# Chunked RWKV recurrence with a fused MLP: pair products and inverses turned by VectorE, and a first state product with 32 stationary columns

## Chip, cores and metric

The kernel runs on one core of one Trainium2 chip. The metric is device time in microseconds (us), the median over repeated runs of the whole kernel, which is one launch.

## What is computed

The reference runs a recurrence over 768 time steps for each of 4 x 8 = 32 heads, with a 40 x 40 state per head, and then a two-layer MLP on the result. Cut to what matters:

```python
for t in range(S):                                          # S = 768
    y[:, :, t] = np.einsum('bhd,bhde->bhe', rt, state)
    Sa = np.einsum('bhde,bhe->bhd', state, at)
    state = state * wt[:, :, None, :] - np.einsum('bhd,bhe->bhde', Sa, bt)
    state = state + np.einsum('bhd,bhe->bhde', vt, kt)
x = y.transpose(0, 2, 1, 3).reshape(B * S, H * D)           # 3072 x 320
h = x @ w_in                                                # 320 x 2048
g = np.where(h >= 1, h, np.where(h <= -1, 0, (h + 1) ** 2 / 4))
return g @ w_out                                            # 2048 x 320
```

All inputs and outputs are float32.

## The kernel before

**The recurrence in chunks.** Time is cut into 24 chunks `c` of 32 steps. Inside a chunk, the products of every step's `a` with every step's `b` form a strictly triangular 32 x 32 matrix per head (the *pair products*). With the inverse of one plus that matrix, a chunk needs only matrix products. Four chunks make a *stage* `s` (six stages), so that pair products and inverses are made for 128 (head, chunk) pairs at once, one per partition.

**Making the pair products and the inverses.** `prelude(s)` multiplies up the decays and writes the scaled rows of k, a, b and the decay product to the DRAM scratch `scr` (the *rows*); for stages 0 and 1 `early_products` does so up front. `ab_set(s)` (`early_ab` for stages 0 and 1) forms the pair products on TensorE, 32 x 32 blocks with time in the partitions, and ScalarE copies them out of PSUM (L206, L303). Then they go to the DRAM tensor `abd` by four DMAs per copy (L208, L306) and come back with one (head, chunk) pair per partition (L316, `lw<-abd`). `invert(s)` runs the elimination: 31 pairs of a multiply (L326) and a subtract (L332) on tile `lw`, on VectorE for stage 0 and on GpSimd for the others. The inverse `W` is written to DRAM tensor `ttd` (L335) and read back, 32 x 32 per head with time in the partitions, into the columns `C_T` of the working tile `cg` (L409, part 1 of `load_cg`, which first drains the stage's inversion: its instructions are written out at the latest there).

**The chain.** `chain(c, hb)` handles a half chunk: 16 of the 32 heads, and 48 of them in all. It has five steps of 16 small products each, on TensorE: L468 (here *the first product*: stationary are the 64 columns of inverse and scores in `cg`, contraction over all 128 partitions, 72 moving columns; ScalarE copies the result to `x0` by L473 in two copies), L479 (*the second product*: the inverse, 32 x 32, times `x0`), L497, L526 and L536. Two half chunks are interleaved. Beside them stand `scores` (L438) and the VectorE transpositions of `turn` (L423, L426, L428), which read rows that `load_ti` brings from `scr` (L274). `load_cg` (L398, L401) brings the other rows.

**The MLP.** Its products (L607 first layer, L581 and L585 second layer) are fed between the chain's steps, 3 x 1024 moving columns per step, from the chunks already done; the correction `gl` (L595) comes from GpSimd.

**What sets the order.** It is written out by hand: the loop at the end takes the chain's steps, ten per chunk, and after each step `background` advances rows, pair products and inversion of the coming stages by the table `WINDOWS`, in counted steps. Inversion of stage 1 has the window from step 16 to 36, the next ones 53 to 72, 90 to 112, 129 to 152 and 170 to 192. Chunk 4 (the first of stage 1) begins at step 40, but its first `load_cg`, with the drain, stands at the start of chunk 3, at step 30. All DMAs but a few go out on SyncE's queue (SP), in program order. Each engine works in order too.

**Before the loop.** Stage 0 is inverted on VectorE, with its output needed by the first half chunk. The order written there is `early_products(0)`, `early_turn(0)`, `early_ab(0)`, the first step of `invert(0)`, `early_products(1)`, and then a loop that takes one inversion instruction at a time with the early work of stage 1 and the first scores between.

Of the kernel before, what the change touches and what calls it, by code (L numbers as in the profile page):

```python
# [23 lines left out]
C_T, C_X, C_R, C_S, C_G, CW = 0, 32, 64, 96, 136, 176  # L24
# [25 lines left out]
def rwkv_moe_kernel(ctx: ExitStack, tc: tile.TileContext, r, k, v, w, a, b, w_in, w_out, ident_d, mask_d, out):  # L50
# [44 lines left out]
    abd = [dram.tile([2, 4, NH // 2, L, L], F32, name=f"abd{s}") for s in range(NS)]  # L95
    ttd = [dram.tile([2, 4, NH // 2, L, L], F32, name=f"ttd{s}") for s in range(NS)]
# [43 lines left out]

    early_rows = {}
# [48 lines left out]
    def early_ab(s, half):  # L190

        ps = psum()
        if half == 0:
            early_rows[s] = work.tile([128, 16, 2, 32], F32, tag="ea", name="ea").rearrange("p a b x -> p (a b x)")
        ab = early_rows[s][:, 512 * half : 512 * half + 512]
# [10 lines left out]
        nc.scalar.copy(ab, ps)  # L206
# [69 lines left out]
    def ab_set(s):  # L276
# [6 lines left out]
        for c in range(4 * s, 4 * s + 4):  # L283
# [18 lines left out]
            ab = work.tile([128, 8, 32], F32, tag="ab", name="ab")  # L302
            nc.scalar.copy(ab, ps[:, 0:256].rearrange("p (s x) -> p s x", x=32))  # L303
            yield AB_W[2]
            for q in range(4):
                nc.sync.dma_start(  # L306
                    abd[c // 4][q // 2, c % 4, q % 2 :: 2].rearrange("h t i -> t h i"), ab[32 * q : 32 * q + 32]
                )
            yield AB_W[3]

    def invert(s):
# [4 lines left out]
        nc.sync.dma_start(Lm, abd[s].rearrange("f c h t i -> (f c h) (t i)"))  # L316
# [4 lines left out]
        L3 = Lm.rearrange("p (t i) -> p t i", i=32)  # L321
# [12 lines left out]
        yield 2  # L334
        nc.sync.dma_start(ttd[s].rearrange("f c h t i -> (f c h) (t i)"), W)  # L335
        yield 3
# [13 lines left out]

    done, size, spent = dict(rows=1, ab=1), dict(rows=10 + 4 * (6.2 + sum(ROWS_W)), ab=AB_W[4] + 4 * (4 * AB_W[0] + sum(AB_W[1:4])), inv=INV_W + 67), {}
# [38 lines left out]
    def load_cg(c, hb, parts=(0, 1)):  # L390
        cg = cgs[(2 * c + hb) % 3]
        hsel = slice(16 * hb, 16 * hb + 16)
        if 0 in parts:
            drain("rows", c // 4)
# [59 lines left out]
    def chain(c, hb):  # L454
# [11 lines left out]
        for h in range(16):  # L466
# [5 lines left out]
            if h % 8 == 7:  # L472
                nc.scalar.copy(x0[:, halves[h // 8]], psv[h // 8][:, :, 0:72])  # L473
# [297 lines left out]
    for hb in range(2):  # L771
        load_ti(0, hb)
        load_cg(0, hb, (0,))
# [152 lines left out]
```

## Time and profile before

| | before |
|---|---|
| runs, us | 974.76, 976.89, 983.64 (median 976.89) |
| span of the profiled execution, us | 974.4 |
| mean granted TensorE clock | 0.850 |
| TensorE busy | 80% |
| VectorE, ScalarE, GpSimd busy | 61%, 49%, 46% |
| DMA packets, MB | 276866, 134.64 |

The span reaches from the first to the last instruction of the program; no other time of that execution is listed. The span stands 0.4 us below the fastest of the three runs and 2.5 us below their median, so sums made against the span are carried to the median by adding 2.5.

In the profile, PE is TensorE's matmul and PEld its weight load, DVE is VectorE, ACT ScalarE, POOL GpSimd and SP SyncE; a q behind the name is the engine's sequencer, which issues DMAs. L468 is line 468 of the kernel. A float32 matmul shows as two records, so that 16 products are "x32". A group's row gives, behind the bar, busy time and the mean of one in ns. A timeline row gives start and length in us; in brackets stands the idle time ahead of it and what ended that. The chain of waits is followed back from the last instruction, at each step to what released it.

### The profile page before, as it was taken

What the parts mean: (1) busy time and instruction counts of PE and PEld (TensorE: products, weight loads), DVE (VectorE), ACT (ScalarE), POOL (GpSimd) and SP (SyncE); (2) the same over time, 40 slices, a digit from 0 to 9 for tenths busy, and PEclk for the clock granted to TensorE, in tenths of its full rate; (3) what the DMA queues carried; (4) which work ended last, traced back from release to release, by engine and by line L of the source; (5) the groups of instructions that cost most, each with busy time, mean ns of one, the idle gap of its engine ahead of it and who ended that gap; (6) DMA issues with size and microseconds to landing.
All of it is one profiled execution on the core that took longest, in us unless ns stands there. A gap on an engine that the chain in (4) does not pass through costs nothing.

```text
span 974.4 us, 35827 instructions
## 1 busy us (share of the span) xinstructions
PE 775.0 (80%) x14976; PEld 692.1 (71%) x14976; DVE 590.4 (61%) x1562; ACT 478.6 (49%) x1230; POOL 443.8 (46%) x673
## 2 busy tenths in 40 slices
PE   4523543447886988799879798989999999999995
PEld 3312532336776887688879687978898899999995
DVE  7782876574756583775654774776665556655321
ACT  5822444212543544454445454546565566656663
POOL 5200223686331599332588232697235962222332
PEclk9755555575997789797999796999999999999998
DMA  8799995565677755896735886856855545552010
GB/s 274 148 193 245 202 207 151 141 139 134 146 156 152 163 138 115 178 186 130 179 100 117 182 160 133 173 135 131 146 115 121 110 101 111 105 90 56 16 36 14
DMA packets 276866, 134.64 MB, mean 138 GB/s; under 512 B 194984, under 2 KB 266856, under 8 KB 276704
## 3 DMA queue, kind: packets, MB, share of 16 engines
q1 hardware_dynamic: 273504, 121.20, 57.9%
q0 software_dynamic: 3200, 11.14, 3.8%
q8 instruction: 118, 1.93, 0.9%
q14 instruction: 44, 0.36, 0.1%
HBM read 96.83 MB, written 33.82 MB: 134 GB/s over the span
## 4 chain that ended last, share of the span: by engine, by line
PE 34%; DMA 16%; POOL 16%; DVE 12%; issue 8%; SPq 8%; ACT 4%; POOLq 0%; ACTq 0%; DVEq 0%
PE ph L607 11%; PE po L581 6%; POOL lw L326 5%; POOL lw L332 4%; DMA ti<-scr 4%; PE po L585 3%; PE p L497 3%; POOL gl L595 3%; SPq L274 3%; PE p L468 3%; PE p L526 2%; DMA ld_a<-in_a_dram 2%; PE p L438 2%; PE p L479 2%; PE p L536 1%
## 5 line engine op out<-in xcount | busy, mean ns | idle before, releaser
L607 PE MATMUL ph<-X,w 120*128 120x256 f32 x1536 | 260.9, 307 | 51.6 <-DVE qt L620 44.3
L595 POOL TENSOR_TENSOR gl<-qt,gh 128x256 fp32r<-128x256 f32 x192 | 140.9, 734 | 280.0 <-ACT gh L594 264.6
L607 PEld LDWEIGHTS ph<-X,w 120*128 120x128 f32 x1536 | 219.8, 203 | 68.1 <-DVE qt L620 51.3
L620 DVE SCALAR_TENSOR_TENSOR qt<-qt,ph 128x256 f32<-128x256 f32 x192 | 79.9, 416 | 150.3 <-ACT qt L614 148.3
L581 PE MATMUL po<-wide,gh 128*128 128x320 f32 x768 | 163.7, 329 | 0.3 <-ACT gh L594 0.3
L594 ACT CAST gh<-qt 128x256 fp32r<-128x256 f32 x192 | 78.0, 406 | 167.6 <-DVE qt L620 166.7
L581 PEld LDWEIGHTS po<-wide,gh 128*128 128x128 f32 x768 | 124.6, 202 | 3.7 <-ACT gh L594 0.5
L613 ACT ACTIVATE qt<-ph,half_c 128x256 f32<-128x256 f32 x192 | 91.1, 474 | 53.4 <-POOL gl L595 39.7
L585 PE MATMUL po<-wide,gl 128*128 128x320 f32 x384 | 99.6, 338 | 17.6 <-POOL gl L595 17.6
L497 PE MATMUL p<-cg 128*64 128x72 f32 (+1 forms) x1536 | 74.8, 262 | 44.2 <-DVE cg L486 39.7
L497 PEld LDWEIGHTS p<-cg 128*64 128x64 f32 x1536 | 66.8, 166 | 54.3 <-ACT cg L490 45.0
L326 POOL TENSOR_TENSOR lw<-lw 128x31 f32<-128x31 f32 (+15 forms) x155 | 94.4, 609 | 18.0 <-DMA lw<-abd 9.3
L490 ACT ACTIVATE cg<-p 32x160 f32<-32x160 f32 x192 | 56.8, 296 | 87.9 <-DVE cg L486 61.0
L447 DVE TENSOR_TENSOR cg<-p,mask 32x256 f32<-32x256 f32 x192 | 80.6, 420 | 25.8 <-PE p L438 23.2
L332 POOL TENSOR_TENSOR lw<-lw 128x31 f32<-128x31 f32 (+15 forms) x155 | 84.1, 543 | 8.8
L504 DVE SCALAR_TENSOR_TENSOR cg<-p,pr 40x160 f32<-40x160 f32 x184 | 59.1, 321 | 41.1 <-PE p L497 39.2
L614 ACT ACTIVATE qt<-qt 128x256 f32<-128x256 f32 x192 | 80.2, 418 | 6.1
L585 PEld LDWEIGHTS po<-wide,gl 128*128 128x128 f32 x384 | 65.6, 197 | 23.9 <-POOL gl L595 21.5
L468 PE MATMUL p<-cg 128*64 128x72 f32 x1536 | 66.4, 243 | 16.7 <-DMA cg<-ttd 15.0
L486 DVE SCALAR_TENSOR_TENSOR cg<-p,mask 32x128 f32<-32x128 f32 x192 | 55.2, 288 | 36.2 <-PE p L479 30.7
L468 PEld LDWEIGHTS p<-cg 128*64 128x64 f32 x1536 | 58.7, 149 | 23.6 <-issue 19.0
L526 PE MATMUL p<-ident,cg 40*64 40x40 f32 x1472 | 57.1, 238 | 1.9 <-issue 1.9
(104 smaller groups left out, 1027.9 us busy)
## 6 DMA issues: line engine op xcount, KB each, us to landing
ti<-scr SPq DMA_DIRECT2D x96, 200.0 KB
ti<-scr SPq DMA_DIRECT2D x96, 168.0 KB
scr<-arena POOLq DMA_DIRECT2D x16, 640.0 KB, 5.4
cg<-scr SPq DMA_DIRECT2D x96, 80.0 KB
X<-Y SPq DMA_DIRECT2D x36, 160.0 KB
scr<-wide SPq DMA_DIRECT2D x8, 640.0 KB
tiab<-scr SPq DMA_DIRECT2D x32, 160.0 KB
scr<-in_r_dram SPq DMA_DIRECT2D x24, 160.0 KB
```

The costliest lines, as they stand in the source:

```text
L326: eng.tensor_mul(t3, W3[:, 0:n, j : j + 1].broadcast_to([128, n, m]), L3[:, j + 1 :, j].unsqueeze(1).broadcast_to([128, n, m]),)
L332: eng.tensor_sub(W3[:, 0:n, j + 1 :], W3[:, 0:n, j + 1 :], t3)
L447: nc.vector.tensor_tensor(out=cg[q, f::2, C_X : C_X + 64][:, 4 * i : 4 * i + 4].rearrange("p h (j x) -> p h j x", x=32), in0=ps[quarter(f, ...
L468: nc.tensor.matmul(psv[h // 8][64 * (1 - f) : 64 * (1 - f) + 64, h // 2 % 4, 0:72], lhsT=cg[:, h, C_T : C_T + 64], rhs=cg[:, h, C_R : C_R ...
L497: nc.tensor.matmul(psv[h // 8][64 * f : 64 * f + 64, h // 2 % 4, 0:n3], lhsT=cgw[:, h * CW + C_G : h * CW + C_G + 64], rhs=cg[:, h, C_R : ...
L581: nc.tensor.matmul(pos[i], lhsT=gh[:, ts_], rhs=w2[f // 8][:, j, f % 8, :], start=f == 0 and j == 0, stop=False)
L585: nc.tensor.matmul(pos[i], lhsT=gl[:, ts_], rhs=w2[f // 8][:, 0, f % 8, :], start=False, stop=f == NF - 1)
L595: nc.gpsimd.tensor_sub(gl, gt, gh.bitcast(F32))
L607: nc.tensor.matmul(ph, lhsT=w1[:, wi, fs], rhs=Xs[g][:, xi, :], start=i == 0, stop=i == 7)
L613: nc.scalar.activation(gt, ph, AF.Relu, bias=half_c, scale=0.5)
L614: nc.scalar.activation(gt, gt, AF.Square)
L620: nc.vector.scalar_tensor_tensor(out=gt, in0=gt, scalar=1.0, in1=ph, op0=ALU.min, op1=ALU.max)
```

## The change

The pair products stay in SBUF: ScalarE copies them into one tile `pairs` (time in the partitions, 32 blocks of 32), and one VectorE transposition of 128 x 1024 (32 x 32 blocks) puts a (head, chunk) pair in each partition, in `lw`. The two time indices of the matrix change places there: the elimination's multiply now reads its second operand with a step of one element, not 32. The inverse leaves `lw` by a second transposition of the same size into the tile `tinv` (in the new function `adopt`), which the second product reads as its stationary operand. `abd` and `ttd` with all their DMAs are gone, and so are the columns `C_T` of `cg`. `adopt(s)` stands at the start of the stage's first chunk (step 40 for stage 1), and the drain of the inversion with it, ten steps later than before. The first product keeps only the 32 columns that are used of its 64; its 16 results go to four quarters of 32 partitions in one PSUM tile, in place of two halves of 64 partitions in two tiles, and one ScalarE copy takes them out. The second product reads four quarters of 32 partitions, not two, and writes one PSUM tile.

```diff
-C_T, C_X, C_R, C_S, C_G, CW = 0, 32, 64, 96, 136, 176
+C_X, C_R, C_S, C_G, CW = 0, 32, 64, 104, 144
...
+    pairs = const.tile([128, 32, 32], F32, name="pairs")
+    tinv = const.tile([128, 4, 8, 32], F32, name="tinv")
+    pairs_f = pairs.rearrange("p m i -> p (m i)")
...
-        nc.scalar.copy(ab, ps)
-        for q in range(4):
-            nc.sync.dma_start(
-                abd[s][q // 2, 2 * half : 2 * half + 2, q % 2 :: 2].rearrange("c h t i -> t (c h) i"),
-                ab[32 * q : 32 * q + 32].rearrange("t (h i) -> t h i", i=32),
-            )
+        nc.scalar.copy(pairs_f[:, 512 * half : 512 * half + 512], ps)
...
-            nc.scalar.copy(ab, ps[:, 0:256].rearrange("p (s x) -> p s x", x=32))
-            yield AB_W[2]
-            for q in range(4):
-                nc.sync.dma_start(
-                    abd[c // 4][q // 2, c % 4, q % 2 :: 2].rearrange("h t i -> t h i"), ab[32 * q : 32 * q + 32]
-                )
-            yield AB_W[3]
+            nc.scalar.copy(pairs_f[:, 256 * (c % 4) : 256 * (c % 4) + 256], ps[:, 0:256])
+            yield AB_W[2] + AB_W[3]
...
-        nc.sync.dma_start(Lm, abd[s].rearrange("f c h t i -> (f c h) (t i)"))
+        nc.vector.transpose(Lm.rearrange("p (i t) -> p i t", t=32), pairs.rearrange("p m i -> p i m"))
...
-        L3 = Lm.rearrange("p (t i) -> p t i", i=32)
+        L3 = Lm.rearrange("p (i t) -> p t i", t=32)
...
-        yield 2
-        nc.sync.dma_start(ttd[s].rearrange("f c h t i -> (f c h) (t i)"), W)
-        yield 3
+        yield 5
+
+    def adopt(s):
+
+        drain("inv", s)
+        W = lw[:, 1024:2048]
+        nc.vector.transpose(tinv.rearrange("p c h i -> p i (c h)"), W.rearrange("p (a i) -> p i a", i=32))
+        turned_out.add(s)
...
-        if 1 in parts:
-            drain("inv", c // 4)
-            for f in range(2):
-                ur = 64 * (1 - f) + 32
-                tt = ttd[c // 4][f, c % 4, 8 * hb : 8 * hb + 8]
-                nc.sync.dma_start(cg[ur : ur + 32, f::2, C_T : C_T + 32], tt.rearrange("h t x -> t h x"))
...
         for h in range(16):
-            f = h % 2
+            f, p = h % 2, h // 2
+            q = 64 * f + 32 * (p % 2)
             nc.tensor.matmul(
-                psv[h // 8][64 * (1 - f) : 64 * (1 - f) + 64, h // 2 % 4, 0:72], lhsT=cg[:, h, C_T : C_T + 64],
-                rhs=cg[:, h, C_R : C_R + 72], start=True, stop=True,
-            )
-            if h % 8 == 7:
-                nc.scalar.copy(x0[:, halves[h // 8]], psv[h // 8][:, :, 0:72])
+                psv[q : q + 32, p // 2, :], lhsT=cg[:, h, C_X : C_X + 32], rhs=cg[:, h, C_R : C_R + 72],
+                start=True, stop=True,
+            )
+        nc.scalar.copy(x0, psv)
         yield
-        psv = psum_2()
-        for p in order:
-            for f in range(2):
-                q = uq[f]
-                nc.tensor.matmul(
-                    psv[p // 4][quarter(f, p // 4), p % 4, 0:72], lhsT=cg[q, 2 * p + f, C_T : C_T + 32],
-                    rhs=x0[q, p, :], start=True, stop=True,
-                )
+        psv = psum()[:, 0:288].rearrange("p (h x) -> p h x", x=72)
+        for h in range(16):
+            f, p = h % 2, h // 2
+            q = 64 * f + 32 * (p % 2)
+            nc.tensor.matmul(
+                psv[quarter(f, p % 2), p // 2, :], lhsT=tinv[q : q + 32, c % 4, 4 * hb + p // 2, :],
+                rhs=x0[q : q + 32, p // 2, :], start=True, stop=True,
+            )
...
-    for hb in range(2):
-        load_cg(0, hb, (1,))
+    adopt(0)
...
+        if 0 < c < NC and c % 4 == 0:
+            adopt(c // 4)
```

The change moves instructions on VectorE and GpSimd. The line numbers shift: in the changed kernel L303 is the transposition of the pair products, L328 that of the inverse, L314 and L320 the elimination's multiply and subtract. The first place is VectorE ahead of stage 0's inversion (`wide` and `ti` are the input and output rows of stages 0 and 1, `arena` scratch). Before:

```order
L172 TENSOR_TENSOR wide_91<-wide_90,arena 128x8x40 x4
L157 COPY wide_90<-ti_80 128x3x40
L158 TENSOR_SCALAR wide_90<-ti_80 128x40
L160 TENSOR_TENSOR wide_90<-wide_90,ti_80 128x4x40 x7
L162 TENSOR_TENSOR wide_90<-wide_90 128x8x40 x3
L167 RECIPROCAL arena<-wide_90 128x4x40
L169 TENSOR_TENSOR arena<-arena,ti_80 128x4x40 x7
L172 TENSOR_TENSOR wide_90<-tiab,arena 128x8x40 x4
L326 TENSOR_TENSOR lw<-lw 128x31
```

And in the changed kernel:

```order
L171 TENSOR_TENSOR wide_91<-wide_90,arena 128x8x40 x4
L303 STREAM_TRANSPOSE lw<-pairs 128x1024
L156 COPY wide_90<-ti_80 128x3x40
L157 TENSOR_SCALAR wide_90<-ti_80 128x40
L159 TENSOR_TENSOR wide_90<-wide_90,ti_80 128x4x40 x7
L161 TENSOR_TENSOR wide_90<-wide_90 128x8x40 x3
L166 RECIPROCAL arena<-wide_90 128x4x40
L168 TENSOR_TENSOR arena<-arena,ti_80 128x4x40 x7
L171 TENSOR_TENSOR wide_90<-tiab,arena 128x8x40 x4
L314 TENSOR_TENSOR lw<-lw 128x31
```

The transposition, which needs stage 0's pair products, stands ahead of all of stage 1's row products (25 instructions), which the DMA did not.

The second place is GpSimd at the end of stage 1's inversion (`ld_a`, `ld_b`, `ld_k`, `rec` and `arena` are rows of stage 2, `gl` is the MLP's). Before:

```order
L326 TENSOR_TENSOR lw<-lw 128x60
L332 TENSOR_TENSOR lw<-lw 128x30x2
L326 TENSOR_TENSOR lw<-lw 128x31
L332 TENSOR_TENSOR lw<-lw 128x31
L255 TENSOR_TENSOR arena<-ld_k,rec 128x8x40
L257 TENSOR_TENSOR arena<-ld_b,rec 128x8x40
L258 DMA scr_100<-arena 128x8x160
L595 TENSOR_TENSOR gl<-qt,gh 128x256
```

And in the changed kernel:

```order
L314 TENSOR_TENSOR lw<-lw 128x231
L320 TENSOR_TENSOR lw<-lw 128x21x11
L246 TENSOR_TENSOR arena<-ld_k,rec 128x8x40
L314 TENSOR_TENSOR lw<-lw 128x220
L248 TENSOR_TENSOR arena<-ld_b,rec 128x8x40
L249 DMA scr_100<-arena 128x8x160
L320 TENSOR_TENSOR lw<-lw 128x22x10
L314 TENSOR_TENSOR lw<-lw 128x207
L582 TENSOR_TENSOR gl<-qt,gh 128x256
```

The last twenty instructions of that inversion, which stood in one block ahead of the rows, now stand between them. In the later stages one instruction of GpSimd's order moves.

The third place is VectorE at the start of chunk 4 (`yt` and `pr` belong to the chain of chunk 3, `ea` to the pair products of stage 2). In the changed kernel:

```order
L496 TENSOR_TENSOR yt<-p_2678,pr_87 128x128
L496 TENSOR_TENSOR yt<-p_2679,pr_87 128x128
L607 SCALAR_TENSOR_TENSOR qt<-qt,ph_63 128x256
L415 STREAM_TRANSPOSE pr_86<-ti_81 128x16x32
L328 STREAM_TRANSPOSE tinv<-lw 128x32x32
L278 STREAM_TRANSPOSE ea<-tiab 128x256 x3
L228 TENSOR_SCALAR arena<-ld_w 128x40
```

The row of `tinv` is new, and the rest stands as before; it waits for GpSimd's last L320 of the stage.

More of the change, by code (lines that the diff above doesn't have):

```diff
@@ L139, in rwkv_moe_kernel @@
     ]
-    early_rows = {}
     def early_load(s):
@@ L192, in early_ab @@
         ps = psum()
-        if half == 0:
-            early_rows[s] = work.tile([128, 16, 2, 32], F32, tag="ea", name="ea").rearrange("p a b x -> p (a b x)")
-        ab = early_rows[s][:, 512 * half : 512 * half + 512]
         for c in (2 * half, 2 * half + 1):
@@ L301, in ab_set @@
                     )
-            ab = work.tile([128, 8, 32], F32, tag="ab", name="ab")
-            nc.scalar.copy(ab, ps[:, 0:256].rearrange("p (s x) -> p s x", x=32))
-            yield AB_W[2]
-            for q in range(4):
-                nc.sync.dma_start(
-                    abd[c // 4][q // 2, c % 4, q % 2 :: 2].rearrange("h t i -> t h i"), ab[32 * q : 32 * q + 32]
-                )
-            yield AB_W[3]
+            assert s - 1 in turned_in
+            nc.scalar.copy(pairs_f[:, 256 * (c % 4) : 256 * (c % 4) + 256], ps[:, 0:256])
+            yield AB_W[2] + AB_W[3]
     def invert(s):
@@ L388, in load_ti, with load_cg @@
         load_rows(tih[hb], c, 0, 200, 16 * hb, 16)
[L390 removed]
+    def load_cg(c, hb):
         cg = cgs[(2 * c + hb) % 3]
         hsel = slice(16 * hb, 16 * hb + 16)
[L393 to L409 removed]
+        drain("rows", c // 4)
+        sc = scr4[c // 4][c % 4][hsel]
+        for f in range(2):
+            vr, ur = 64 * (1 - f), 64 * (1 - f) + 32
+            nc.sync.dma_start(
+                cg[vr : vr + 32, f::2, C_S : C_S + 80], sc[f::2, :, O_V : O_V + 80].rearrange("h t x -> t h x")
+            )
+            nc.sync.dma_start(
+                cg[ur : ur + 32, f::2, C_G : C_G + D], sc[f::2, :, O_B : O_B + D].rearrange("h t x -> t h x")
+            )
     evs = {}
@@ L474, in chain @@
+        nc.scalar.copy(x0, psv)
         yield
-        psv = psum_2()
-        for p in order:
-            for f in range(2):
-                q = uq[f]
-                nc.tensor.matmul(
-                    psv[p // 4][quarter(f, p // 4), p % 4, 0:72], lhsT=cg[q, 2 * p + f, C_T : C_T + 32],
-                    rhs=x0[q, p, :], start=True, stop=True,
-                )
+        psv = psum()[:, 0:288].rearrange("p (h x) -> p h x", x=72)
+        for h in range(16):
[4 more added lines that the diff above has]
+                rhs=x0[q : q + 32, p // 2, :], start=True, stop=True,
+            )
@@ L483, in chain @@
         for i in range(2):
             for f in range(2):
-                q = uq[f]
+                q, j = uq[f], 1 - i
                 nc.vector.scalar_tensor_tensor(
-                    out=cg[q, f::2, C_R : C_R + 32][:, halves[i]], in0=psv[i][quarter(f, i), :, 0:32], scalar=-1.0,
+                    out=cg[q, f + 2 * i :: 4, C_R : C_R + 32], in0=psv[quarter(f, i), :, 0:32], scalar=-1.0,
                     in1=mask[quarter(f, i)].unsqueeze(1).broadcast_to([32, 4, 32]), op0=ALU.mult, op1=ALU.mult,
@@ L489, in chain @@
                 )
-                nc.scalar.mul(cg[q, f::2, C_S : C_S + D][:, halves[1 - i]], psv[1 - i][quarter(f, 1 - i), :, 32:72], -1.0)
+                nc.scalar.mul(cg[q, f + 2 * j :: 4, C_S : C_S + D], psv[quarter(f, j), :, 32:72], -1.0)
         yield
```

15 lines of the change are left out of this document (5 added, 10 removed).

## The prediction

> **What bounds the kernel now.** I read the page first: busy shares, DMA slices, and the chain of waits by engine.
>
> ```profile
> span 974.4 us, 35827 instructions
> PE 775.0 (80%) x14976; PEld 692.1 (71%) x14976; DVE 590.4 (61%) x1562; ACT 478.6 (49%) x1230; POOL 443.8 (46%) x673
> DMA  8799995565677755896735886856855545552010
> PE 34%; DMA 16%; POOL 16%; DVE 12%; issue 8%; SPq 8%; ACT 4%; POOLq 0%; ACTq 0%; DVEq 0%
> ```
>
> No engine bounds the whole: on the chain that ended last PE has a third, while DMA, SP's issuing and GpSimd have 40% together. So I split the span with the table by stretches.
>
> ```profile
> 100.00:200.00 100.00, 44.71 (x1072) 40.42 (x1069) 67.40 (x163) 37.75 (x90) 38.00 (x57) 0.59 0.78 178
> 600.00:700.00 100.00, 95.26 (x1899) 85.02 (x1898) 69.43 (x186) 54.49 (x146) 65.29 (x104) 0.96 0.66 138
> 800.00:900.00 100.00, 100.00 (x2013) 91.11 (x2012) 60.38 (x161) 62.15 (x164) 26.70 (x37) 1.00 0.45 90
> ```
>
> The first number behind the length is PE's busy time. Early, PE works 45 of 100 us at a granted clock of 0.59, with the DMA engines 78% busy: loads and order of arrival decide. From 600 on PE is busy 95% and more, at 800 without rest and at clock 1.00: there only shorter PE work helps. Third, PE's timeline of a late half chunk:
>
> ```profile
> 869.82 1.07 PEld L468 LDWEIGHTS p<-cg 128*64 128x64 f32 x32
> 869.82 1.22 PE L468 MATMUL p<-cg 128*64 128x72 f32 x32
> 870.97 0.39 PE L607 MATMUL ph<-X,w 120*128 120x256 f32 x1
> 872.92 0.48 PE L438 MATMUL p<-pr,ev 40*32 40x32 f32 x32
> 873.33 1.13 PE L526 MATMUL p<-ident,cg 40*64 40x40 f32 x32
> 875.93 0.70 PE L479 MATMUL p<-x,cg 32*32 32x72 f32 x32
> 876.57 1.22 PE L607 MATMUL ph<-X,w 120*128 120x256 f32 x8
> 883.54 0.66 PE L468 MATMUL p<-cg 128*64 128x72 f32 x14
> ```
>
> A half chunk takes 883.54 - 869.82 = 13.7 us, 2.7 us per step. A group's cost is the distance to the next start: the first product 870.97 - 869.82 = 1.15 us (36 ns per record), the second 0.64 us (20 ns) with the same 72 moving columns.
>
> **Term 1, ahead of the loop.** The timeline there:
>
> ```profile
> 18.80 0.27 DVE L157 COPY wide<-ti 128x120 f32<-128x120 f32 x1
> 27.76 0.59 ACT L206 COPY ea<-p 128x512 f32<-128x512 f32 x1 [3.49 <-PE p L202]
> 28.18 4.38 DVE L172 TENSOR_TENSOR wide<-tiab,arena 128x320 f32<-128x320 f32 x4
> 32.19 0.35 SPq L316 DMA_DIRECT2D lw<-abd  x1
> 36.23 0.21 DVE L326 TENSOR_TENSOR lw<-lw 128x31 f32<-128x31 f32 x1 [3.67 <-DMA lw<-abd]
> 72.83 0.22 DVE L332 TENSOR_TENSOR lw<-lw 128x31 f32<-128x31 f32 x1
> 73.08 0.34 SPq L335 DMA_DIRECT2D ttd<-lw  x1
> 81.42 6.70 SPq L215 DMA_DIRECT2D scr<-wide  x4
> 82.19 1.73 PE L479 MATMUL p<-x,cg 32*32 32x72 f32 x32
> 88.17 2.36 SPq L672 DMA_DIRECT2D lw<-in_moe_w_out_dram  x2
> ```
>
> Stage 1's row products ran on VectorE from 18.80 to 32.56, 13.8 us, while the pair products were made and sent. Now the transposition stands ahead of them and waits for ScalarE's copy, which ends at 28.35. What a transposition costs I take from these rows (with the elimination's, for term 4):
>
> ```profile
> L423 DVE STREAM_TRANSPOSE cg<-ti 64x256 f32<-64x256 f32 x96 | 42.0, 438 | 1.2
> L428 DVE STREAM_TRANSPOSE pr<-ti 128x512 f32<-128x512 f32 x48 | 33.6, 701 | 0.0
> L326 DVE TENSOR_TENSOR lw<-lw 128x255 f32<-128x255 f32 x2 | 1.2, 608 | 0.1
> L332 DVE TENSOR_TENSOR lw<-lw 128x255 f32<-128x255 f32 x2 | 0.8, 424 | 0.1
> L326 POOL TENSOR_TENSOR lw<-lw 128x255 f32<-128x255 f32 x10 | 7.8, 776 | 0.4
> L332 POOL TENSOR_TENSOR lw<-lw 128x255 f32<-128x255 f32 x10 | 6.8, 683 | 0.5
> ```
>
> From 256 to 512 elements 263 ns are added, so 1024 cost 701 + 2 x 263 = 1.23 us. Its operands step by 32 elements; the multiply that reads so (608 ns) runs at 1.43 times the subtract (424), so 1.8 us is the upper bound. VectorE is then free for the row products at about 29.7, and the elimination starts at 29.7 + 13.8 = 43.5, where it stood at 36.23: **7.3 us later**. It lasted 72.83 + 0.22 - 36.23 = 36.8 us. Its 31 multiplies now read contiguously; at 255 elements the two groups differ by 184 ns, at few elements by nothing, so some 4 us at most fall away: an end between 76.5 and 80.3, with the second transposition 78 to 82. Before, write and read through DRAM came next, and then the first product, which now needs no inverse: L479 stood at 82.19. On that path 0 to 4 us are won. SP wins more: it stood at L335 and behind it for the inversion, sent stage 1's rows only from 81.42 and the weights to `lw` at 88.17; the rows can now go from about 73, the weights from 80 to 82, when the second transposition has left `lw`. I take **-5** (-1 to -8).
>
> **Term 2, landings on the chain.** Two round trips stand on the chain in the loop:
>
> ```profile
> 299.24 3.21 DMA abd<-ab
> 739.36 3.65 DMA lw<-abd
> 276.15 0.75 SPq L306
> 221.16 0.71 POOL lw L326
> 231.71 0.43 POOL lw L326
> ```
>
> 3.21 + 3.65 us go; the transpositions in their place are in term 6. **-7** (0 to -7, since the next arrival may be as late).
>
> **Term 3, the first product.** With 32 stationary columns in four quarters I take the second product's row, 0.64 us: its 72 moving columns and four quarters are the same, its contraction is shorter. Saved are 0.51 us per half chunk. Where PE is the limit, from 600 to 900 us, lie 300 / 13.7 = 22 half chunks: 22 x 0.51 = **-11**. Bounds: 0 (unchanged at 1.15) and 48 x 0.51 = -24. Ahead of 600 PE idles often enough that I count nothing there. The copy to `x0` is one in place of two, but starts only behind all 16 products; I count it at nothing, since PE has the MLP's products from 870.97 until L479 starts at 875.93. Without that cover the path would gain or lose less than one copy.
>
> The Trainium skill, TensorE: Matmul & The Clock Gate, section "Part 3: Packing small matmuls — row/col tiling", says that a weight load overlaps a running matmul only when it is in other row groups, and here all quarters use all rows. By that rule the term would be 0. The trace does not agree with it for two halves: L468's weight loads, over all rows, were busy 1.07 us inside the 1.22 us of its own products. For quarters no run yet shows it; it is the first rival below.
>
> **Term 4, GpSimd.** The multiply's excess over the subtract, 776 - 683 = 93 ns at 255 elements, is up to 2 us per inversion; five of them, about half on the chain: -4. The tail of stage 1's inversion stood on the chain from 221.16 to 231.71 in one block and is now spread among the rows. Together **-4** (0 to -13).
>
> **Term 5, queue and traffic.**
>
> ```profile
> L409 SPq DMA_DIRECT2D cg<-ttd x96: 302/449/1693, 77.9 to 885.5; - x96
> L306 SPq DMA_DIRECT2D abd<-ab x64: 302/449/2018, 275.6 to 726.6; - x64
> SPq L409 <- DMA ttd<-lw: 20.3, 6, 4.4
> DMA packets 276866, 134.64 MB, mean 138 GB/s; under 512 B 194984, under 2 KB 266856, under 8 KB 276704
> ```
>
> With 16 of L208, 6 of L316 and 6 of L335, 188 of SP's 946 issues go (20%), and SP no longer stands at L409 for 20 us in six waits, with all later loads behind it. Six stages each write and read two tensors of 128 x 1024 x 4 B: 12.6 of 134.64 MB, 9%. On the chain SP's issuing has 8%, 78 us, and DMA 16%, 156 us. A fifth of the one is 16, 9% of the other 14. SP's issues stand back to back on the chain (the run that begins with the row 276.15), so I take nearly all of the first and a quarter of the second: **-18** (0 to -30).
>
> **Term 6, what is added.** Ten transpositions in the loop, 1.23 to 1.8 us each, 12 to 18 us of VectorE. VectorE is 61% busy and has 12% of the chain, so one busy us in five counts: 2 to 4 us. Each also waits: for ScalarE's last copy of the pair products, or for GpSimd's last subtract. Behind it on VectorE stand L447, L486 and L504, for which PE waits. I allow 2 us more: **+5** (0 to +20).
>
> **Sum.** -5 - 7 - 11 - 4 - 18 + 5 = -40: a span of 934.4, a median of 934.4 + 2.5 = **936.9 us**. Its own range is 915 to 955.
>
> **The rivals.** *The first product gains nothing*, because its quarters share all rows: 936.9 + 11 = 948. For it: L468 before, with all rows, costs 36 ns per record, L479 20 ns. Against it: halves of 64 columns and quarters of 32 differ too.
>
> *The next limit takes over*: without DMAs and queue, the loop waits for GpSimd's and VectorE's order instead, which keep their work. Terms 2 and 5 give nothing, 936.9 + 25 = 962. For it: GpSimd has 16% of the chain.
>
> *VectorE stands for GpSimd* (the slower side). At `adopt`, VectorE waits for GpSimd's last subtract of the stage, with all of the chain's VectorE work behind it. Each us there costs five, and past 8 us per stage the 40 are gone; at 12 the time is 936.9 + 60 = 997. Against it: the inversion's window ends 4 steps ahead of `adopt(1)` and 8 ahead of the others, at 2.7 us per step 11 to 22 us of room.
>
> *The second product's quarters take turns.* Its four row quarters now write one PSUM tile. Were they to run one after another, each record would cost four times 20 ns, a half chunk 3 x 0.64 = 1.92 us more, 48 of them 92: 936.9 + 92 = 1029 us. Against it: L438's two row halves write one tile too, and 32 of its records take 873.33 - 872.92 = 0.41 us, 13 ns each, less than L479's 20 over two tiles: no sign of turns.
>
> The Trainium skill, TensorEngine Tiling (Array Packing), section "Restrictions and Gotchas", says that different row tiles cannot access the same PSUM bank at once, which would give this case. L438's 13 ns speak against it for two row tiles; no run yet shows four.
>
> **How the numbers follow.** Forecast 0.70; first product without gain 0.12; next limit 0.09; VectorE stands 0.06; quarters take turns 0.03. A measurement here can tell about 1% from no change, so faster means under 967.1. The first two cases are faster, and the third half of the time: 0.87. The other half of it is the same, 0.04, and the last two are slower, 0.09. The range is 908 to 964: from the forecast with term 5 whole and term 3 at its bound, to the third case.
>
> **What would show it.** Right: no L409 or L306 on SP; 128 x 1024 transpositions of 1.2 to 1.8 us; the elimination of stage 0 starting near 43; a late half chunk of 13.2 us with the first product 0.65 us to the next start. Wrong: tinv's row idle for more than 8 us ahead of it; a first product still at 1.15; a second product above 1 us; or PE as idle as before between 100 and 600.

## The result: 941 us, and the profile after

The changed kernel took 941.36 us, the median of four runs (939.1 to 945.44), beside 980.26 us (974.76 to 987.69) for the kernel before on the same chip: a ratio of 0.9594, with a 95% interval of 0.9528 to 0.9661. The profiled execution took 939.9 us with a span of 937.4, at a mean granted clock of 0.862. The page of the changed kernel, in the order in which the prediction read the other one:

```profile
span 937.4 us, 35480 instructions
PE 740.5 (79%) x14976; PEld 654.3 (70%) x14976; DVE 606.9 (65%) x1574; ACT 456.3 (49%) x1182; POOL 428.4 (46%) x673
DMA packets 223167, 122.01 MB, mean 130 GB/s; under 512 B 142825, under 2 KB 214697, under 8 KB 223009
PE 37%; DVE 23%; DMA 12%; POOL 8%; ACT 7%; issue 6%; SPq 6%; DVEq 0%; ACTq 0%; POOLq 0%
```

On the chain, the last row, DMA, SP's issuing and GpSimd fell from 40% to 26%, as argued. But VectorE rose from 12 to 23% and ScalarE from 4 to 7%: something new stands there. The table by stretches, with PE's busy time behind the length; first a row of the kernel before:

```profile
200.00:300.00 100.00, 72.28 (x1317) 63.54 (x1318) 63.68 (x179) 38.23 (x103) 51.36 (x76) 0.81 0.67 144
```

And the changed kernel:

```profile
100.00:200.00 100.00, 38.00 (x942) 33.08 (x938) 68.98 (x165) 34.47 (x83) 42.07 (x64) 0.57 0.76 166
200.00:300.00 100.00, 86.02 (x1621) 75.49 (x1622) 69.56 (x195) 42.28 (x114) 48.81 (x74) 0.81 0.75 162
800.00:900.00 100.00, 97.69 (x1751) 88.57 (x1751) 49.58 (x133) 61.88 (x164) 29.54 (x41) 1.00 0.25 57
```

From 100 to 200 us PE stays idle for most of the time (38 us busy), with the DMA engines 76% busy. From 200 to 300 it is now busy 86 us where it was 72. The timeline of PE and of its weight loads in a late half chunk:

```profile
833.79 0.53 PEld L456 LDWEIGHTS p<-cg 128*32 128x32 f32 x32
833.79 0.71 PE L456 MATMUL p<-cg 128*32 128x72 f32 x32
834.43 0.39 PE L594 MATMUL ph<-X,w 120*128 120x256 f32 x1
839.38 0.70 PE L466 MATMUL p<-x,tinv 32*32 32x72 f32 x32
840.02 1.22 PE L594 MATMUL ph<-X,w 120*128 120x256 f32 x8
847.10 0.71 PE L456 MATMUL p<-cg 128*32 128x72 f32 x32
```

The first product (L456) has 834.43 - 833.79 = 0.64 us to the next start, 0.51 less than before, and the second product (L466) still has 0.64. The half chunk takes 847.10 - 833.79 = 13.3 us, 0.4 less. Ahead of the loop, the timelines of VectorE, PE and SP:

```profile
29.17 1.94 DVE L303 STREAM_TRANSPOSE lw<-pairs 128x1024 f32<-128x1024 f32 x1 [10.03 <-ACT pairs L202]
44.68 0.18 DVE L314 TENSOR_TENSOR lw<-lw 128x31 f32<-128x31 f32 x1
75.25 7.03 SPq L206 DMA_DIRECT2D scr<-wide  x4
78.86 1.96 DVE L328 STREAM_TRANSPOSE tinv<-lw 128x1024 f32<-128x1024 f32 x1
80.97 1.18 PE L466 MATMUL p<-x,tinv 32*32 32x72 f32 x32 [8.73 <-DVE tinv L328]
82.34 2.53 SPq L659 DMA_DIRECT2D lw<-in_moe_w_out_dram  x2
```

The elimination starts at 44.7, the inverse is turned at 80.8, the second product starts 1.2 us earlier than before, SP's rows and weights 6 us earlier. Behind it, the third to the sixth half chunk begin 4.6 to 6.7 us earlier than before. In the loop, VectorE never stands for the transposition of the inverse; the last number of its group is the idle time ahead of it:

```profile
L328 DVE STREAM_TRANSPOSE tinv<-lw 128x1024 f32<-128x1024 f32 x6 | 12.1, 2018 | 0.0
```

What the prediction did not foresee stands in the waits of VectorE and ScalarE (total, times, longest). Before:

```profile
ACT cg L490 <- DVE cg L486: 61.0, 20, 11.0
```

And in the changed kernel:

```profile
ACT cg L477 <- DVE cg L473: 149.5, 192, 10.0
DVE cg L473 <- ACT cg L477: 52.0, 144, 0.4
```

The eight instructions that take the second product's results out of PSUM, four on each engine, ran side by side; now each but the first waits for the one ahead of it on the other engine. The changed kernel's timeline shows the turns:

```profile
85.22 0.29 DVE L473 SCALAR_TENSOR_TENSOR cg<-p,mask 32x128 f32<-32x128 f32 x1
85.54 0.30 ACT L477 ACTIVATE cg<-p 32x160 f32<-32x160 f32 x1 [2.96 <-DVE cg L473]
85.87 0.28 DVE L473 SCALAR_TENSOR_TENSOR cg<-p,mask 32x128 f32<-32x128 f32 x1 [0.36 <-ACT cg L477]
```

### The profile page after: what moved, and what is told of

The parts are those of the page before. It is cut to its first block, busy times and chain, and to the rows that moved or that the text cites. A ratio compares the mean times of both kernels' runs of the same rounds, so it can differ in the third digit from the quotient of the medians.

```text
span 937.4 us, 35480 instructions
## 1 busy us (share of the span) xinstructions
PE 740.5 (79%) x14976; PEld 654.3 (70%) x14976; DVE 606.9 (65%) x1574; ACT 456.3 (49%) x1182; POOL 428.4 (46%) x673
## 4 chain that ended last, share of the span: by engine, by line
PE 37%; DVE 23%; DMA 12%; POOL 8%; ACT 7%; issue 6%; SPq 6%; DVEq 0%; ACTq 0%; POOLq 0%
PE ph L594 12%; PE po L568 7%; PE p L484 4%; PE po L572 4%; DVE arena L234 3%; PE p L513 3%; DVE cg L473 3%; SPq L265 3%; DVE qt L607 2%; DVE rec L243 2%; ACT cg L477 2%; POOL lw L314 2%; POOL lw L320 2%; DMA ti<-scr 2%; DMA ld_a<-in_a_dram 2%
## 5 line engine op out<-in xcount | busy, mean ns | idle before, releaser
L594 PEld LDWEIGHTS ph<-X,w 120*128 120x128 f32 x1536 | 215.4, 200 | 83.0 <-DVE qt L607 67.9
L484 PE MATMUL p<-cg 128*64 128x72 f32 (+1 forms) x1536 | 74.4, 259 | 44.2 <-ACT cg L477 43.5
L484 PEld LDWEIGHTS p<-cg 128*64 128x64 f32 x1536 | 65.6, 163 | 55.0 <-ACT cg L477 46.0
L600 ACT ACTIVATE qt<-ph,half_c 128x256 f32<-128x256 f32 x192 | 90.9, 473 | 20.2 <-POOL gl L582 14.3
L320 POOL TENSOR_TENSOR lw<-lw 128x31 f32<-128x31 f32 (+15 forms) x155 | 83.7, 540 | 8.3
L314 POOL TENSOR_TENSOR lw<-lw 128x31 f32<-128x31 f32 (+15 forms) x155 | 78.8, 509 | 8.5
L513 PEld LDWEIGHTS p<-ident,cg 40*64 40x64 f32 x1472 | 51.8, 146 | 3.6 <-issue 1.6
L466 PE MATMUL p<-x,tinv 32*32 32x72 f32 x1536 | 38.5, 242 | 10.8 <-DVE tinv L328 8.7
```

The source lines that it names most:

```text
L314: eng.tensor_mul(t3, W3[:, 0:n, j : j + 1].broadcast_to([128, n, m]), L3[:, j + 1 :, j].unsqueeze(1).broadcast_to([128, n, m]),)
L320: eng.tensor_sub(W3[:, 0:n, j + 1 :], W3[:, 0:n, j + 1 :], t3)
L484: nc.tensor.matmul(psv[h // 8][64 * f : 64 * f + 64, h // 2 % 4, 0:n3], lhsT=cgw[:, h * CW + C_G : h * CW + C_G + 64], rhs=cg[:, h, C_R : ...
L513: nc.tensor.matmul(pst[64 * f : 64 * f + 64, p, :], lhsT=cn[er[f], h, C_S : C_S + 64], rhs=ident[er[f]], start=True, stop=True)
L594: nc.tensor.matmul(ph, lhsT=w1[:, wi, fs], rhs=Xs[g][:, xi, :], start=i == 0, stop=i == 7)
L600: nc.scalar.activation(gt, ph, AF.Relu, bias=half_c, scale=0.5)
```

## The experiments

Twelve versions ran, each beside the kernel before on the same chip, whose median was 976 to 978 us in these runs. Unless said otherwise a version is the changed kernel with one edit, shown cut to the lines that matter. Ratios are to the kernel before, with a 95% interval in brackets. Differences between versions are differences of medians: the four runs of the changed kernel alone spread over 6 us, so a difference of a few us says little.

**The turns: addresses or tile?** The two engines write the same tile `cg` with interleaved heads now, and read one PSUM tile. The first version gives whole halves of the pairs to the quarters, so that the written columns are separate ranges as before:

```diff
-            q = 64 * f + 32 * (p % 2)
+            q = 64 * f + 32 * (p // 4)
...
-                    out=cg[q, f + 2 * i :: 4, C_R : C_R + 32], in0=psv[quarter(f, i), :, 0:32], scalar=-1.0,
+                    out=cg[q, f::2, C_R : C_R + 32][:, halves[i]], in0=psv[quarter(f, i), :, 0:32], scalar=-1.0,
```

> The changed kernel with one thing different: the 8 pairs of heads of a half chunk go to the partition quarters by halves (pairs 0 to 3, pairs 4 to 7) and not by turns (even, odd). The eight instructions behind the second product (four of VectorE, four of ScalarE) then write heads 0 to 7 or 8 to 15 as before the change, not every fourth head; there is still one PSUM tile. Theory: in the changed kernel these eight run strictly in turn (2.6 us from first to last, before the change 1.3) because the address ranges of every fourth head interleave, so that each write waits for the other engine's. It expects 1.3 us again, ScalarE's wait for VectorE there down from 149.5 to about 61 us, VectorE's wait for ScalarE from 52 to about 0, and 10 to 25 us less in all, since the chain is short of time ahead of 600 us: 917 to 932. Rival one: the turns come from the one PSUM tile that both engines read; then nothing changes (2.6 us, 941). Rival two: the turns go, but the chain has other waits in the place; 1.3 us and 938 to 943.

It took 941.61 us (936.61 to 947.08), 0.9643 (0.9606 to 0.9681). The waits:

```profile
ACT cg L476 <- DVE cg L472: 145.9, 192, 9.1
DVE cg L472 <- ACT cg L476: 52.0, 144, 0.4
```

Nothing moved, so the theory of the interleaved addresses fell. The other version keeps the interleaving and puts the second product's results in two PSUM tiles by the parity of the pair:

```diff
-        psv = psum()[:, 0:288].rearrange("p (h x) -> p h x", x=72)
+        psv = [psum()[:, 0:288].rearrange("p (h x) -> p h x", x=72) for _ in range(2)]
...
-                psv[quarter(f, p % 2), p // 2, :], lhsT=tinv[q : q + 32, c % 4, 4 * hb + p // 2, :],
+                psv[p % 2][quarter(f, p % 2), p // 2, :], lhsT=tinv[q : q + 32, c % 4, 4 * hb + p // 2, :],
```

> The changed kernel with the second product's results in two PSUM tiles, as before the change, and the heads in turns as in the changed kernel. Theory (interleaved address ranges of the heads): still 2.6 us from the first to the last of the eight instructions, the two waits near 149 and 52 us, time within 3 us of 941. Rival (the shared PSUM tile): 1.3 us and both waits gone as in the run before.

One run took 918.59 us. Its waits, with no row the other way round:

```profile
ACT cg L477 <- DVE cg L473: 58.7, 19, 9.2
```

The shared PSUM tile made the turns, and they cost 941.36 - 918.59 = 22.8 us. The program shows it: with one tile each of ScalarE's four instructions is told to wait for VectorE, with two tiles one of the four. So the order is written in the program; whether the chip would serve both engines at once out of one tile no run here shows.

**The stand ahead of stage 1's rows.** The first step of stage 0's inversion, with its transposition, is moved behind stage 1's row products:

```diff
-    step_back("inv", 0)
     early_products(1)
+    step_back("inv", 0)
```

> The changed kernel with the first step of stage 0's inversion (the transposition of its pair products and the setting of the unit matrix) written behind stage 1's row products and not ahead of them. Theory: the transposition held VectorE from about 19 to 29 us; without that the elimination starts near 35 in place of 44, the inverse is turned at about 71 in place of 79, and the loop comes 7 to 9 us earlier; of this 4 to 9 us are left at the end: 932 to 937. Rival: the first half chunks wait for loads (weights and rows) that do not come earlier, so the gain is gone within the first chunks: 939 to 943, with the same first start but the same times from chunk 3 on.

935.88 us (931.07 to 937.34), 0.957 (0.9541 to 0.96). Its timeline:

```profile
32.56 1.90 DVE L303 STREAM_TRANSPOSE lw<-pairs 128x1024 f32<-128x1024 f32 x1
34.56 0.19 DVE L314 TENSOR_TENSOR lw<-lw 128x31 f32<-128x31 f32 x1
73.26 1.18 PE L466 MATMUL p<-x,tinv 32*32 32x72 f32 x32 [8.72 <-DVE tinv L328]
```

The second product starts 7.7 us earlier, and 941.36 - 935.88 = 5.5 us of it are there at the end.

**The first product: quarters or columns?** The 16 products of L456 are issued for the even pairs first, then for the odd ones, so that two quarters take turns at a time, not four:

```diff
-        for h in range(16):
-            f, p = h % 2, h // 2
-            q = 64 * f + 32 * (p % 2)
+        for n in range(16):
+            f, p = n % 2, 2 * (n // 2 % 4) + n // 8
+            h, q = 2 * p + f, 64 * f + 32 * (p % 2)
```

> The changed kernel with only the order of the first product's 16 products different: the even pairs first, then the odd ones, so that two quarters take turns at a time and not four; 32 stationary columns each, as before. Theory A (the number of quarters in turn sets the pace): 32 records take 1.1 to 1.2 us again in a late half chunk, in place of 0.70, and the time rises by 8 to 12 us to about 950. Theory B (the number of stationary columns sets it): 0.70 us as in the changed kernel, 941.

947.64 us (942.68 to 950.97), 0.9694 (0.9657 to 0.9732). PE's timeline:

```profile
844.10 0.98 PE L456 MATMUL p<-cg 128*32 128x72 f32 x32
845.01 0.39 PE L594 MATMUL ph<-X,w 120*128 120x256 f32 x1
```

The slot is 0.91 us, 28 ns per record: halfway between the 20 ns of four quarters in turn and the 36 ns of two halves with 64 columns. Neither theory holds alone; both the number of quarters in turn and the columns count. The kernel loses 6.3 us for 0.27 us per half chunk, which is 0.27 x 23: it fits the term's factor of 22, as far as a difference of 6 us can tell.

**Both repairs.** Two PSUM tiles and the late transposition together:

> The changed kernel with both edits that helped: the second product's results in two PSUM tiles, and stage 0's first transposition behind stage 1's row products. Theory: the two act at different places (the eight instructions behind each second product; the time ahead of the loop), so the gains add up: 918.6 less 5.5 is 913, between 908 and 918, with VectorE's wait for ScalarE behind the second product at 0 and the elimination of stage 0 starting near 34.6. Rival: with the chain faster, the earlier start meets loads that are not there yet, and the sum is 917 to 921.

915.69 us (913.41 to 919.25), 0.9368 (0.9335 to 0.9401), the fastest version. Against the late transposition alone the two tiles bring 935.88 - 915.69 = 20.2 us, which agrees with the single run above.

**The price of issues and packets.** 160 small transfers that wait for nothing are added on SP, each 32 KB in packets of 128 bytes; they write to a DRAM tensor that nobody reads:

```diff
+    def send(n):
+        for _ in range(n):
+            q = sent[0] % 4
+            nc.sync.dma_start(
+                junk[sent[0]], mask[32 * q : 32 * q + 32].unsqueeze(1).broadcast_to([32, 8, 32])
+            )
+            sent[0] += 1
```

> The changed kernel with the DMA work of the old layout changes put back without their waits: 2 DMAs of 32 x 8 x 128 bytes on SyncE's queue behind each half chunk's other loads (96) and 4 behind each of the 16 later pair products (64). They read a constant and write a DRAM tensor that nobody reads, so that nothing waits for them; only the issue time (160 of them) and the small packets are there again, about three quarters of the issues and two fifths of the small packets' bytes come from this. Theory: the room on the queue and in the DMA engines was worth the predicted 18 us, and most of it comes back as loss: 951 to 962. Rival: the queue has room, and what counted was the standing of the queue at the landings and waits: 939 to 945.

957.63 us (953.74 to 963.2), 0.98 (0.9754 to 0.9846): 16.3 us more (20 by the ratios), 0.1 us for each, issue and packets together. The 160 are 85% of the 188 that the change removed.

**Each layout change undone.** First the pair products go through DRAM again, with the four writes per copy and the read of the kernel before; the elimination then also reads with the old step of 32:

```diff
-        nc.vector.transpose(Lm.rearrange("p (i t) -> p i t", t=32), pairs.rearrange("p m i -> p i m"))
+        nc.sync.dma_start(Lm, abd[s].rearrange("q c h t i -> (q c h) (t i)"))
...
-        L3 = Lm.rearrange("p (i t) -> p t i", t=32)
+        L3 = Lm.rearrange("p (t i) -> p t i", i=32)
```

> The changed kernel with one half of its layout change undone: the pair products go to DRAM and come back by DMA as before the change (80 small writes, 6 reads), the elimination reads with the old step of 32 elements, and the inverse is still turned by VectorE. Theory (the predicted terms): the landings on the chain cost 7, GpSimd's slower multiplies 2 to 4, the writes' share of queue and traffic 6 to 9; against that VectorE does not stand ahead of stage 1's row products (4 to 6 gained, by the run with the late transposition): 947 to 957. Rival: this half gave nothing in the sum: 938 to 944.

952.86 us (950.81 to 953.98), 0.9745 (0.9706 to 0.9783): 11.5 us more, as expected. But two things were undone there. So the old step was put back alone, with the transposition kept:

```diff
-        nc.vector.transpose(Lm.rearrange("p (i t) -> p i t", t=32), pairs.rearrange("p m i -> p i m"))
+        nc.vector.transpose(Lm.rearrange("p (t i) -> p i t", i=32), pairs.rearrange("p m i -> p i m"))
...
-        L3 = Lm.rearrange("p (i t) -> p t i", t=32)
+        L3 = Lm.rearrange("p (t i) -> p t i", i=32)
```

> The transposition of the pair products puts the time indices down as before, so that the elimination's multiply reads its second operand with a step of 32 elements again; nothing else differs from the changed kernel. Term 4 says that the faster multiply is worth 4 us, half of it in the inversions and half by the order: if so, GpSimd's multiply at 255 elements takes 776 ns again, and the time is 943 to 946 us. The rival, that the inversions are hidden, gives 941 to 942. The transposition itself, which writes 32 elements apart now, should keep its 1.9 to 2.0 us.

955.75 us (946.52 to 957.0), 0.9719 (0.9669 to 0.977), above both ranges: 14.4 us by the medians, 12 by the ratios, three times what term 4 allowed. The groups of the changed kernel, GpSimd's multiply (L314) and subtract (L320) at 255 elements:

```profile
L314 POOL TENSOR_TENSOR lw<-lw 128x255 f32<-128x255 f32 x10 | 6.5, 648 | 0.4
L320 POOL TENSOR_TENSOR lw<-lw 128x255 f32<-128x255 f32 x10 | 6.8, 683 | 0.5
L314 POOL TENSOR_TENSOR lw<-lw 128x31 f32<-128x31 f32 (+15 forms) x155 | 78.8, 509 | 8.5
```

And with the old step:

```profile
L314 POOL TENSOR_TENSOR lw<-lw 128x255 f32<-128x255 f32 x10 | 7.8, 777 | 0.4
L314 POOL TENSOR_TENSOR lw<-lw 128x31 f32<-128x31 f32 (+15 forms) x155 | 94.1, 607 | 8.5
PE 39%; DVE 23%; POOL 11%; DMA 10%; ACT 7%; issue 6%; SPq 4%; DVEq 0%; ACTq 0%; POOLq 0%
```

GpSimd works 94.1 - 78.8 = 15.3 us longer in its five inversions, and on the chain it has 11% in place of 8%: about 30 us more. Another part stands ahead of the loop, where VectorE inverts stage 0: from the elimination's first multiply to the second transposition it takes 81.15 - 44.84 = 36.3 us with the old step and 78.86 - 44.68 = 34.2 in the changed kernel.

So the step alone explains the run before it: between the old step with the transposition (955.75) and the old step with the DRAM path (952.86) no difference can be measured (2.9 us by the medians, 2.5 the other way by the ratios, and the intervals overlap). The DRAM path has no transposition standing ahead of stage 1's rows, which was worth 5.5 us above. If that counts in full here, the pair products' round trip costs some 3 to 8 us; the noise allows as much again either way.

Then the inverse goes through DRAM again, written once and read by four DMAs at the stage's first chunk:

```diff
-        nc.vector.transpose(tinv.rearrange("p c h i -> p i (c h)"), W.rearrange("p (a i) -> p i a", i=32))
+        for q in range(4):
+            nc.sync.dma_start(tinv[32 * q : 32 * q + 32], ttd[s][q].rearrange("c h t i -> t c h i"))
```

> The changed kernel with the other half undone in part: the inverse goes to DRAM by one DMA per stage and comes back into the same tile by four (where the kernel before had 16 per stage), pair products turned by VectorE as in the changed kernel. Theory: SyncE's queue stands behind the inversion again (one write and the read behind it, 5 stages), with loads behind it, while the queue's issues stay few: 943 to 952. Rival: what counted of the inverse's way were the 96 issues into the working tile, not the standing: 939 to 943.

972.1 us (965.56 to 975.72), 0.9944 (0.9908 to 0.998): 30.7 us more, far above the theory. Its waits, and its timeline where SP's rows of stage 1 (L207) and the second product (L469) of chunk 4 stand:

```profile
PE p L469 <- DMA tinv<-ttd: 29.9, 18, 11.6
```

```profile
86.03 6.74 SPq L207 DMA_DIRECT2D scr<-wide  x4
265.21 0.28 PE L469 MATMUL p<-x,tinv 32*32 32x72 f32 x2 [3.43 <-DMA tinv<-ttd]
```

PE waits 29.9 us for the reads where it waits 8.7 for the transposition, and SP's rows go out at 86.03, not 75.25. Some 8 of the 31 us are there at the start already: the second half chunk's first product begins at 97.97, in the changed kernel at 89.94. The landing seemed to be the cause, so the next version reads one chunk at a time, a chunk ahead of its use, as the kernel before did; the inversion is then written out ten steps earlier:

```diff
+    def load_t(c):
+        drain("inv", c // 4)
+        for q in range(4):
+            nc.sync.dma_start(
+                tinvs[c % 3][32 * q : 32 * q + 32], ttd[c // 4][q, c % 4].rearrange("h t i -> t h i")
+            )
```

> The inverse goes through DRAM again, but a chunk at a time into one of three tiles and a chunk ahead of its use, as in the kernel before, with the inversion written out ten steps earlier. Theory: most of the 30.7 us of the version that read all of a stage's inverse at its first chunk came from the second product standing for that read; then this version takes 946 to 956 us (its issues and packets alone, priced by the 160 extra transfers at 0.1 us each, cost about 10). Rival: the traffic and SP's queue made them, wherever the reads stand; then it takes 965 to 975, with 96 reads in place of 24 rather more.

978.18 us (972.22 to 983.8), 0.9984 (0.9952 to 1.0016): slower still, and the theory of the late read fell. PE's wait for the reads is all but gone in the loop (the longest is the one ahead of it), yet SP now stands for the write, as it did before the change:

```profile
PE p L473 <- DMA tinv<-ttd: 12.0, 3, 11.2
SPq L332 <- DMA ttd<-lw: 19.8, 6, 4.0
```

```profile
200.00:300.00 100.00, 76.71 (x1408) 67.46 (x1400) 61.17 (x177) 34.54 (x93) 52.95 (x81) 0.77 0.66 147
```

```profile
84.80 6.72 SPq L207 DMA_DIRECT2D scr<-wide  x4
96.61 1.19 PE L463 MATMUL p<-cg 128*32 128x72 f32 x32
```

The second half chunk's first product starts at 96.61 (89.94 in the changed kernel, 91.16 before), and from 200 to 300 PE does 76.7 us of work where the changed kernel does 86.0. Whichever way the inverse came through DRAM, it cost 31 to 37 us; PE waits if it is read late, SP with all loads behind it if early. How much of the second is SP's six waits, how much the 72 further issues and how much the earlier inversion was not separated by runs, but the traces show one place where the earlier inversion counts. It is the way from the seventh half chunk's first product to the eighth's, at the end of stage 1's inversion; before, in this version and in the changed kernel:

```profile
213.69 1.22 PE L468 MATMUL p<-cg 128*64 128x72 f32 x32
245.98 1.22 PE L468 MATMUL p<-cg 128*64 128x72 f32 x32
```

```profile
223.34 0.71 PE L463 MATMUL p<-cg 128*32 128x72 f32 x32
252.62 1.19 PE L463 MATMUL p<-cg 128*32 128x72 f32 x32
```

```profile
206.64 0.71 PE L456 MATMUL p<-cg 128*32 128x72 f32 x32
228.81 1.19 PE L456 MATMUL p<-cg 128*32 128x72 f32 x32
```

That is 32.3, 29.3 and 22.2 us. All versions whose inversion is written out ten steps later take 21 to 24 us here, the one with the late read too (22.3); the two further ones below, whose inversion ends early, take 30 to 33. In this version GpSimd's elimination stands on the chain from 228.1 to 240.1 in one block, much as it did before the change. So some 7 of its 37 us, and 10 of the whole change's gain, arise where the inversion ends and not from the way through DRAM; no run moved that end alone.

**The products alone.** Both layouts through DRAM, the inverse a chunk ahead; what stays of the change is the first product in four quarters and the second in one PSUM tile:

> Both layout changes go through DRAM as in the kernel before, the inverse a chunk ahead: what is left of the change is the first product with 32 columns in four quarters and the second product in one PSUM tile. Theory, terms added up: 976 - 11 to 17 (first product) + 22 (the turns of the eight instructions behind the second product, by the version with two tiles) = 981 to 987 us, no faster than the kernel before. Rival: the turns cost less where loads and the queue set the pace early, and the products alone bring 5 to 11: 965 to 971.

989.61 us (984.29 to 994.0), 1.0114 (1.0081 to 1.0147), above both ranges: this half of the change makes the kernel 11 us slower. The same with two PSUM tiles for the second product:

> As the version with the products alone, with the second product's results in two PSUM tiles by pair parity. Theory: the turns are gone, 22 us less than the version with the products alone, 959 to 965 us, which is the first product's own gain of 11 to 17. Rival: the turns are hidden behind the loads' waits; then the two versions differ by under 10 us.

977.74 us (975.61 to 986.39), 0.9997 (0.9964 to 1.003), between the two: the turns cost 11.9 us here. PE's timeline of this last version:

```profile
879.20 0.71 PE L475 MATMUL p<-cg 128*32 128x72 f32 x32
879.84 0.39 PE L613 MATMUL ph<-X,w 120*128 120x256 f32 x1
892.42 0.71 PE L475 MATMUL p<-cg 128*32 128x72 f32 x32
```

A late half chunk takes 13.2 us, 0.5 less than before, and 22 of them 11 us; the whole gains nothing all the same. What takes the 11 us back is open: the profiled execution took 986.39 us, 8.7 above the median, at a granted clock of 0.91 from 600 to 800 us (0.96 and 0.98 before), so its trace can't tell where a median run loses them.

## Why the prediction was right, point by point

The predicted 936.9 us and the direction were right, and most of the mechanisms with them. That the sum came so close was partly luck: a loss that the prediction did not see (term 6) was about as large as gains that it had too small (term 4) or in the wrong place (term 5). Three steps from the kernel before to the changed one, by the medians of the versions:

| step | us |
|---|---|
| products alone (978.4 to 989.61) | +11 |
| pair products turned, elimination with contiguous reads (989.61 to 978.18) | -11 |
| inverse turned, inversion ended ten steps later (978.18 to 941.36) | -37 |

**Term 1, ahead of the loop (-5).** The elimination began at 44.7, not 43.5, because the transposition began 0.8 us later and took 1.94 us, not 1.23; it ended at 78.8, inside the predicted 76.5 to 80.3. That the elimination begins later was counted at 7.3 us and made good by the second round trip that falls away; moving the transposition showed that 5.5 us could be had beside that. The half chunks behind it began 4.6 to 6.7 us earlier, as the term says. That SP would win most was right: the versions with the inverse in DRAM sent those rows at 84.8 and 86.0.

**Terms 2 and 5, landings, queue and traffic (-7 and -18).** The price of an issue with its packets was right: 160 of them cost 16.3 us, and term 5 has 18 for 188. But the gain was put on the count of issues of both tensors together, and the runs put nearly all of it on one: the pair products with their 86 issues were worth some 3 to 8 us, the inverse with its 102 was worth 37, of which some 7 are the inversion's earlier end, and even with 30 it was worth 31. A reason that was argued and not tried: the inverse's way lies between the end of an inversion and the first product that needs it, and PE or SP stands there, as the waits show. For the pair products in DRAM GpSimd, ScalarE and, ahead of the loop, VectorE stand, 5.9, 3.9 and 3.7 us. Together the three terms -5, -7 and -18 make -30, and 37 less 7 is 30 too.

**Term 3, the first product (-11).** The slot shrank by the predicted 0.51 us, the half chunk by 0.4, so 22 half chunks would give 9 us. The version with two quarters at a time speaks for it in the whole (6.3 us for 0.27); the last version, which kept the short slot and gained nothing, does not. The rival by which the slot stays at 1.15 us is refuted: all quarters use all 128 rows, and a record costs 20 ns with four quarters in turn, 28 with two. The sentence of the Trainium skill, TensorE: Matmul & The Clock Gate, section "Part 3: Packing small matmuls — row/col tiling", that a weight load overlaps a running matmul only from other row groups is not borne out by L456, whose weight loads were busy 0.53 us within the 0.71 us of its products. The same section of the Trainium skill also lets a load into the background weight buffer go ahead of running matmuls; no run here shows whether that is what happened.

**Term 4, GpSimd (-4).** Mis-sized by a factor of three or more. At 255 elements the multiply fell from 776 to 648 ns, where 683 was expected, and the step was worth 12 to 14 us in the whole, where the term took about half of 10. Some 2 of them arise on VectorE ahead of the loop (36.3 to 34.2 us); the other 10 to 12 are most of GpSimd's 15.3. The tail of stage 1's inversion, which the term counted too, was worth some 7 to 10 us by the traces. With both the bound of -13 did not hold.

**Term 6, what is added (+5).** This is the term that failed. The transpositions in the loop took 2.0 us, above the bound of 1.8. The rival *VectorE stands for GpSimd* did not come: the row of `tinv` has no idle time ahead of it. What their 20 us on VectorE cost in the whole was not tried alone. What cost 20 to 23 us was an edit that the prediction valued at nothing: one PSUM tile in place of two behind the second product. It asked whether TensorE's quarters would take turns in that tile; they do not (0.64 us as before, so that the rule of the Trainium skill, TensorEngine Tiling (Array Packing), section "Restrictions and Gotchas", against several row tiles in one PSUM bank at once shows no sign here with four row tiles, each of which writes 32 partitions of its own). The engines that read the tile do take turns.

**The range and the rivals.** The range's lower end is added up wrongly: term 5 whole and term 3 at its bound give 936.9 - 12 - 13 = 911.9, not 908. The rival *the next limit takes over* (962) spoke of GpSimd's and VectorE's order. In part it is what happened: VectorE and ScalarE took over 14 points of the chain from DMA, SP and GpSimd. About six of them are the turns, since with two PSUM tiles the chain reads:

```profile
PE 40%; DVE 20%; DMA 13%; POOL 10%; SPq 6%; issue 6%; ACT 4%; DVEq 0%; ACTq 0%; POOLq 0%
```

Without the turns the same change gives 919 us (the single run).

The terms with their measured sizes, -30 for terms 1, 2 and 5, -9 for term 3, -13 and -7 for term 4 and +22 for term 6, sum to -37; measured were -35 to -39, by the median of the kernel before that is taken. So near a sum is no proof of its parts: the -9 is worked out from the slot and the -7 from one place of the traces. Nor are they independent: the turns cost 12 us with the layouts in DRAM and 20 to 23 without.

## What to carry to other kernels

When results are packed into fewer PSUM tiles, look at who reads them: two engines that took results out side by side may be ordered one behind the other, and the program's waits show it before any run. A round trip through DRAM is not priced by its bytes or issues alone: of two with the same bytes one was worth some 30 us here, the other about 5. The waits point to what stands behind a round trip until it lands. An elementwise operand with a long step slowed the longer multiplies of every inversion, and the change of layout that made it contiguous was worth more than the transfers of the pair products that went with it. When a change moves where a piece of work ends in the program's order, that is an edit of its own: look for it in the traces.

## What the runs showed of the hardware

A 32 x 32 block transposition of 128 x 1024 float32 took 1.90 to 2.08 us, 2.8 times the 0.70 us of 128 x 512. All of the larger ones read with a step of 32 elements and the smaller ones read 32 elements in a row, so size and step are not separated; writing with that step or without took 1.96 to 2.02 us in the mean. A float32 multiply with one operand at a step of 32 elements took 602 to 612 ns on VectorE and 776 to 785 ns on GpSimd at 255 elements; contiguous, 424 and 648. Sixteen products over all 128 rows with 32 stationary columns took 20 ns per record with four column quarters in turn and 28 with two.
